# Windowed attention on one core: weighted values with the queries on the partitions, one column more for the row sums, and results that return through HBM by transposing loads

## The chip, the cores and the metric

The kernel runs on one core of one Trainium2 chip. The metric is the device time of one execution in microseconds (us), the median of several runs. All matrix operands are bf16; sums are kept in f32.

## The reference

Two attention blocks over the same x (1 x 2048 x 1024, 32 heads of 32) are mixed by a gate for each token. Block A is linear attention; block B is attention over eight earlier tokens, two apart. The change touches only block B.

```python
# block A (short): a = (phi(q) @ (phi(k)^T v)) / (phi(q) . sum phi(k)), then @ A_wo
# block B
qkv = x @ B_wqkv                         # q, k, v: 32 heads of 32
idx = pos[:, None] - 2 * arange(8)       # the token itself and 7 before it, 2 apart
logits = einsum("bhsd,bhswd->bhsw", q, k[idx]) * 32 ** -0.5   # masked where idx < 0
attn = softmax(logits)
b = einsum("bhsw,bhswd->bhsd", attn, v[idx]).reshape(B, S, D) @ B_wo
g = sigmoid((x * gate_w).sum(-1))
out = g * a + (1 - g) * b
```

## The kernel before

**Layout.** The tokens are split by parity into two halves of 1024, so that a window of stride 2 becomes eight neighbours within one half. `xT`, `qT`, `kT` hold features on the partitions (128 x 8 x 2048). `ps_all` is the whole of PSUM, eight banks of 128 x 512 f32.

**Stages.** TensorE (PE) goes through: (1) 50 warming matmuls (L1392); (2) the values of block B, x tile by x tile, each bank moved to a `vst` buffer and stored to `vB_hbm` (L1407 to L1419); (3) the keys and queries of block B, even half and then odd half (L1527 to L1543); (4) the keys of block A, `pkS` (L1577); (5) the state of block A (L1640; its small matmuls, called kv, L1627); (6) queries, fold and output, x tile by x tile (L1735 on), where one group of matmuls multiplies `qT`, which by then holds the result of block B, by `B_wo` (L1720).

**The fills.** Block B's attention is cut in 18 fills of 114 queries (two groups of 57, or 56 in the last of a half) against two groups of 64 keys. They are threaded between the big matmuls of stages 3 to 5: `slot` is called after each group of eight big matmuls, and starts a fill every fifth time (`FILL = 0.2`). A fill (`fill`, L1452) consists of:
- two loads of 64 rows of values from `vB_hbm` into a `v` buffer, one of three (L1458);
- `spread` (L1444): the queries are copied from `qT` to `qx`, for the even heads on ScalarE (ACT) and the odd heads on VectorE (DVE), with zeros elsewhere;
- **S** (L1467): 32 matmuls, 64 keys by 114 columns, into the four banks `SO` (4 to 7);
- the exponential on ACT (L1472) and the mask on DVE (L1475), both on `E`, 128 x 1824, keys on the partitions;
- three slots later **PV** (`values`, L1481): 64 matmuls (L1488) with the values as weights (64 keys x 32) and the exponentials as moving data (57 columns), and 8 matmuls (L1494) with ones as weights and 456 columns of exponentials, for the row sums; the result has head features on the partitions;
- logarithm (L1503) and exponential of the negative (L1504) of the sums on ACT, and the product on DVE (L1505), twice, each for half of the features. The product goes into `qT`, over the queries that the fill has used.

**Order.** Each operation is given to a planner (`Prog`, L63) with a cost and its dependencies. It simulates the five queues by those costs and so fixes the order of the instructions on each engine; a `move` from PSUM goes to ACT or DVE, whichever it reckons will be done first. On the chip every engine runs its list in that order, and SyncE (SP) issues nearly all DMAs, also in order.

Of the kernel before, what the change touches and what calls it, by code (L numbers as in the profile page):

```python
# [1119 lines left out]
def build_kernel(nc, A_x, A_wqkv, A_wo, B_x, B_wqkv, B_wo, gate_w, out):  # L1120
    del B_x
    S = A_x.shape[1]
# [45 lines left out]
    ps = ps_guard.__enter__()  # L1168
# [19 lines left out]

    def hb(p0, p1, half):
        return [("H%d" % half, p0, p1, None)]  # L1190

    xT = SB([128, 8, S], BF16, "xT")
    qT = SB([128, 8, S], BF16, "qT")
# [6 lines left out]
    ones = SB([128, 128], BF16, "ones")  # L1200
# [30 lines left out]
    prodr = Ring([SB([128, 1024], F32, "prod%d" % i, at=Er.t[0].lo + 4096 * i) for i in range(2)])  # L1231
# [18 lines left out]

    FILL = 0.2
    PVLAG = 3
    SUMS_AT = 2
    WARM = 50
    PASSES = 6
    mm = lambda n: max(n / 2400.0, 0.0267) + 0.0025
# [3 lines left out]
    def plan(seen):  # L1260
# [119 lines left out]
        def move(dst, src, n, bank, reg, scale=None, reads=()):  # L1380

            if scale is None:
                fd = lambda e: e.tensor_copy(dst, src())  # L1383
                fa = lambda e: e.activation(dst, src(), ACT.Copy)  # L1384
            else:
                fd = lambda e: e.tensor_scalar(dst, src(), scale, None, op0=ALU.mult)  # L1386
                fa = lambda e: e.activation(dst, src(), ACT.Copy, scale=scale)
            P.op("any", {"act": fa, "dve": fd}, {"act": act(n) + (0.1 if reads else 0.0), "dve": dps(n)}, reads=[bank.iv] + list(reads), writes=[reg])
# [9 lines left out]
        for b in range(NT // 4):  # L1398
            for half in range(2):
# [4 lines left out]
                else:  # L1404
                    steps += [[(4 * b + i, half, 0, 8)] for i in range(4)]
        open_ = {}
        for t, half, lo, hi in [p for q in steps for p in q]:  # L1407
# [8 lines left out]
            vt, vs = vst.next()  # L1416
            move(vt[:, :], bank.ap, 512, bank, vt.all())
            P.op("sp", lambda e, t=t, vt=vt, half=half: e.dma_start(vB_hbm[t * 128:(t + 1) * 128, half * 512:half * 512 + 512], vt[:, :]), 0.6, reads=[vt.all()],
                 writes=[hb(t * 128, (t + 1) * 128, half)], chan="vst%d" % vs, lat=0.5, prio=5)  # L1419
            if (t, half) in early:  # L1420
                load_w(*early[t, half], after=[o])
# [18 lines left out]
        slot_n = [0]  # L1440

        ready = []

        def spread(e_, qs, nq, offs):  # L1444
            ready.append((e_, qs))
# [6 lines left out]
        def fill(e_, qs, nq, offs):  # L1452
            t0 = e_ * HS
            k0 = [qs + nq * h - offs[h] for h in range(2)]
            m = msk[KINDS.index((nq, offs))]
            vt, vslot = vr.next()
            for h in range(2):
                P.op("sp", lambda e, h=h: e.dma_start(vt[64 * h:64 * h + 64, :], vB_hbm[t0 + k0[h]:t0 + k0[h] + 64, :]), 0.4,  # L1458
                     reads=[hb(t0 + k0[h], t0 + k0[h] + 64, i) for i in range(2)], writes=[vt.all()], chan="v%d_%d" % (vslot, h), lat=0.5)
            if (e_, qs) not in ready:  # L1460
                spread(e_, qs, nq, offs)

            def s_fn(e):
                for c in range(8):
                    for h in range(2):
                        for g in range(2):
                            last = e.matmul(SO[2 * g + c // 4].ap(c % 4 * 2 * nq, (c % 4 + 1) * 2 * nq)[64 * h:64 * h + 64, :], kT[64 * g:64 * g + 64, c, t0 + k0[h]:t0 + k0[h] + 64],  # L1467
                                            qx[64 * g:64 * g + 64, :, c, h * nq:(h + 1) * nq], start=True, stop=True, tile_position=(64 * g, 64 * h))
# [12 lines left out]
            def values():  # L1481

                def each(e):
                    for c in range(8):
                        for j in range(4):
                            for h in range(2):
                                hd = 4 * c + j
                                last = e.matmul(SO[h].ap(c * nq, (c + 1) * nq)[32 * j:32 * j + 32, :], vt[64 * h:64 * h + 64, hd * 32:hd * 32 + 32],  # L1488
                                         E[64 * h:64 * h + 64, (j // 2 * 16 + 2 * c + j % 2) * nq:(j // 2 * 16 + 2 * c + j % 2 + 1) * nq],
                                         start=True, stop=True, tile_position=(64 * h, 32 * j))  # L1490
                        if c == SUMS_AT:
                            for j in range(4):
                                for h in range(2):
                                    e.matmul(SO[2 + h].ap(0, 8 * nq)[32 * j:32 * j + 32, :], ones[64 * h:64 * h + 64, 0:32],  # L1494
                                             E[64 * h:64 * h + 64, j // 2 * 16 * nq:(j // 2 + 1) * 16 * nq].rearrange("p (c s q) -> p c s q", c=8, s=2)[:, :, j % 2, :],
                                             start=True, stop=True, tile_position=(64 * h, 32 * j))
                    return last
                bi = [s.iv for s in SO]
                P.op("pe", each, 0.66, mode="c", reads=[vt.all(), ones.all(), E.all()], writes=bi, name="PV")
                for g in range(2):  # L1500
                    L, _ = Lr.next()
                    pb = lambda o, g=g: ps[:, 4 + 2 * o:6 + 2 * o, 4 * g * nq:4 * (g + 1) * nq]
                    P.op("act", lambda e, L=L, pb=pb: e.activation(L[:, :, 0:4 * nq], pb(1), ACT.Ln), act(8 * nq), reads=[SO[2].iv, SO[3].iv], writes=[L.all()])  # L1503
                    P.op("act", lambda e, L=L: e.activation(L[:, :, 0:4 * nq], L[:, :, 0:4 * nq], ACT.Exp, scale=-1.0), act(8 * nq), reads=[L.all()], writes=[L.all()])  # L1504
                    P.op("dve", lambda e, L=L, pb=pb, g=g: e.tensor_tensor(  # L1505
                        qT[:, 4 * g:4 * g + 4, t0 + qs:t0 + qs + 2 * nq].rearrange("p c (h q) -> p h c q", h=2),
                        pb(0).rearrange("p h (c q) -> p h c q", c=4), L[:, :, 0:4 * nq].rearrange("p h (c q) -> p h c q", c=4), ALU.mult), dps(8 * nq),
                        reads=[SO[0].iv, SO[1].iv, L.all()], writes=[qT.part((4 * g, 4 * g + 4), (t0 + qs, t0 + qs + 2 * nq))])
            after(PVLAG, values)

        pace = [0.0]
# [334 lines left out]
```

## Time and profile before

| | |
|---|---|
| median of 3 runs | 484.11 us (483.94 to 484.77) |
| the profiled execution | 484.96 us, of which its span is 483.1 us |
| PE busy | 472.1 us, 98% |
| DVE busy | 304.8 us, 63% |
| ACT busy | 162.1 us, 34% |
| DMA engines, hardware queue q1 | 33.8% of 16 engines' span |
| granted TensorE clock | 1.000 |

Times in the views are microseconds from the start of the span. PE is the matmul side of TensorE, PEld its weight loads, which overlap matmuls. A matmul's duration holds its passage through the array, so that neighbours overlap: the distance of their starts is what they cost. In a row of the timeline several instructions are merged: the start of the first, the time to the end of the last, and their number; so the last one started at start + time - duration of one. `SPq` is the DMA-issuing queue of SP. In a group of instructions the numbers after the bar are busy time, mean ns of one, and the idle time before them with what ended it. Some matmul records are missing.

### The profile page before, as it was taken

What the parts mean: (1) busy time and instruction counts of PE and PEld (TensorE: products, weight loads), DVE (VectorE), ACT (ScalarE), POOL (GpSimd) and SP (SyncE); (2) the same over time, 40 slices, a digit from 0 to 9 for tenths busy, and PEclk for the clock granted to TensorE, in tenths of its full rate; (3) what the DMA queues carried; (4) which work ended last, traced back from release to release, by engine and by line L of the source; (5) the groups of instructions that cost most, each with busy time, mean ns of one, the idle gap of its engine ahead of it and who ended that gap; (6) DMA issues with size and microseconds to landing.
All of it is one profiled execution on the core that took longest, in us unless ns stands there. A gap on an engine that the chain in (4) does not pass through costs nothing.

```text
span 483.1 us, 9788 instructions
## 1 busy us (share of the span) xinstructions
PE 472.1 (98%) x4241; PEld 227.2 (47%) x4306; DVE 304.8 (63%) x514; ACT 162.1 (34%) x246; POOL 39.4 (8%) x40
## 2 busy tenths in 40 slices
PE   9999999999999999999999999999999999999997
PEld 6444444444444444444544445444444444444444
DVE  2121276799877778777743334489987777777522
ACT  1111111112344447677754466364222000011000
POOL 3000000000000000000025656010000000000000
PEclk9999999999999999999999999999999999999999
DMA  8999995232100032103004430461232111121111
GB/s 235 212 205 296 372 357 153 67 108 87 45 25 23 23 111 78 34 27 107 24 25 121 138 94 3 133 198 35 57 103 68 43 45 43 47 82 48 45 43 48
DMA packets 73973, 48.43 MB, mean 100 GB/s; under 512 B 38337, under 2 KB 67394, under 8 KB 73922
## 3 DMA queue, kind: packets, MB, share of 16 engines
q1 hardware_dynamic: 73090, 46.94, 33.8%
q10 hardware_dynamic: 832, 0.79, 0.7%
q8 instruction: 35, 0.57, 0.5%
q14 instruction: 16, 0.13, 0.1%
HBM read 30.41 MB, written 8.39 MB: 80 GB/s over the span
## 4 chain that ended last, share of the span: by engine, by line
PE 98%; issue 1%; DVE 0%
PE ps_all L1356 57%; PE ps_all L1720 23%; PE ps_all L1648 11%; PE ps_all L1467 2%; PE ps_all L1488 2%; PE ps_all L1392 1%; PE ps_all L1494 1%; PE ps_all L1627 1%; PE ps_all L1675 0%; DVE o L1386 0%
## 5 line engine op out<-in xcount | busy, mean ns | idle before, releaser
L1356 PE MATMUL ps_all<-w,xT 128*128 128x512 bf16 x493 | 109.5, 379 | 2.4 <-issue 2.1
L1356 PE MATMUL ps_all<-xT,w 128*128 128x512 bf16 x497 | 110.1, 379 | 1.6 <-issue 1.3
L1356 PEld LDWEIGHTS ps_all<-xT,w 128*128 128x128 bf16 x512 | 49.4, 98 | 58.8
L1356 PEld LDWEIGHTS ps_all<-w,xT 128*128 128x128 bf16 x512 | 49.0, 98 | 57.9
L1362 ACT ACTIVATE e<-ps_all 128x512 bf16<-128x512 f32 x64 | 38.1, 596 | 104.7 <-PE ps_all L1356 103.1
L1720 PE MATMUL ps_all<-w,qT 128*128 128x512 bf16 (+1 forms) x261 | 60.5, 373 | 0.2
L1720 PE MATMUL ps_all<-kT,aT 128*128 128x512 bf16 (+1 forms) x257 | 60.0, 372 | 0.4
L1356 PE MATMUL ps_all<-kT,xT 128*128 128x512 bf16 x249 | 57.0, 379 | 0.6 <-issue 0.3
L1648 PE MATMUL ps_all<-pk,xn 128*128 128x512 bf16 x242 | 55.5, 379 | 1.7 <-issue 1.4
L1383 DVE CAST vst<-ps_all 128x512 bf16<-128x512 f32 x16 | 11.1, 692 | 45.7 <-PE ps_all L1356 45.7
L1720 PEld LDWEIGHTS ps_all<-w,qT 128*128 128x128 bf16 x264 | 25.7, 98 | 29.7 <-issue 0.2
L1720 PEld LDWEIGHTS ps_all<-kT,aT 128*128 128x128 bf16 x264 | 25.8, 98 | 29.4
L1356 PEld LDWEIGHTS ps_all<-kT,xT 128*128 128x128 bf16 x256 | 24.7, 98 | 30.0 <-issue 0.7
L1386 DVE TENSOR_SCALAR o<-ps_all,gm 128x512 bf16<-128x512 f32 (+1 forms) x27 | 19.7, 731 | 28.0 <-PE ps_all L1720 28.0
L1648 PEld LDWEIGHTS ps_all<-pk,xn 128*128 128x128 bf16 x256 | 23.9, 98 | 27.7
L1472 ACT ACTIVATE E<-ps_all 128x1824 bf16<-128x1824 f32 (+1 forms) x18 | 30.4, 1687 | 15.8 <-PE ps_all L1467 15.8
L1505 DVE TENSOR_TENSOR qT<-ps_all,L 128x456 bf16<-128x456 f32 (+1 forms) x36 | 21.1, 625 | 20.4 <-ACT L L1504 20.2
L1363 DVE TENSOR_SCALAR e<-e 128x512 bf16<-128x512 bf16 x64 | 19.0, 299 | 23.0 <-ACT e L1362 22.8
L1610 POOL TENSOR_TENSOR zacc<-zacc,pk 128x1024 f32<-128x1024 f32 x15 | 32.0, 2131 | 17.0 <-DVE E L1475 16.2
L1384 ACT ACTIVATE vst<-ps_all 128x512 bf16<-128x512 f32 x16 | 9.6, 597 | 49.4 <-PE ps_all L1356 49.4
L1384 ACT ACTIVATE kT<-ps_all 128x512 bf16<-128x512 f32 x25 | 14.2, 600 | 31.7 <-PE ps_all L1356 31.7
L1475 DVE TENSOR_TENSOR E<-E,msk 128x1824 bf16<-128x1824 bf16 (+1 forms) x18 | 19.8, 1102 | 5.9 <-ACT E L1472 5.9
(67 smaller groups left out, 386.8 us busy)
## 6 DMA issues: line engine op xcount, KB each, us to landing
v<-vB_hbm SPq DMA_DIRECT2D x36, 128.0 KB, 2.6
vB_hbm<-vst SPq DMA_DIRECT2D x32, 128.0 KB, 4.9
w<-in_B_wqkv_dram SPq DMA_DIRECT2D x4, 1024.0 KB, 8.1
xt<-in_A_x_dram SPq DMA_DIRECT2D x16, 256.0 KB, 4.8
w<-in_A_wqkv_dram SPq DMA_DIRECT2D x4, 1024.0 KB, 9.2
xn<-in_A_x_dram SPq DMA_DIRECT2D x8, 512.0 KB, 4.1
out_dram<-o SPq DMA_DIRECT2D x15, 256.0 KB, 2.0
kT<-in_A_wqkv_dram SPq DMA_DIRECT2D x2, 1024.0 KB, 5.4
```

The costliest lines, as they stand in the source:

```text
L1356: last = e.matmul(bank.ap(), lhs(dc), rhs(dc), start=(dc == 0), stop=(dc == 7))
L1362: P.op("act", lambda e: e.activation(e_[:, :], bank.ap(), ACT.Exp), act(512), reads=[bank.iv], writes=[e_.all()])
L1363: P.op("dve", lambda e: e.tensor_scalar(e_[:, :], e_[:, :], 1.0, 1e-6, op0=ALU.min, op1=ALU.add), 0.25, reads=[e_.all()], writes=[e_.all()])
L1383: fd = lambda e: e.tensor_copy(dst, src())
L1384: fa = lambda e: e.activation(dst, src(), ACT.Copy)
L1386: fd = lambda e: e.tensor_scalar(dst, src(), scale, None, op0=ALU.mult)
L1472: P.op("act", lambda e: e.activation(E[:, 0:32 * nq].rearrange("p (j q) -> p j q", j=4), ps[:, 4:8, 0:8 * nq], ACT.Exp), act(32 * nq), rea ...
L1475: mk = P.op("dve", lambda e: e.tensor_tensor(ev(), ev(), m[:, :, :].rearrange("p r q -> p (r q)")[:, None, :].to_broadcast([128, 16, 2 * n ...
L1505: P.op("dve", lambda e, L=L, pb=pb, g=g: e.tensor_tensor(qT[:, 4 * g:4 * g + 4, t0 + qs:t0 + qs + 2 * nq].rearrange("p c (h q) -> p h c q" ...
L1610: P.op("pool", lambda e, t=t: e.tensor_tensor(zacc[:, :], zacc[:, :], pkS[:, t, :], ALU.add), 2.2, reads=[src, zacc.all()], writes=[zacc.a ...
L1648: last = e.matmul(bank.ap(), tl[:, t, cs:cs + 128], pkS[:, t, r * 512:(r + 1) * 512], start=(t == 0), stop=(t == NT - 1))
L1720: last = e.matmul(bank.ap(0, f1 - f0), lh[:, k, t * 128:(t + 1) * 128], w[:, k, f0:f1], start=(first and k == 0), stop=(not first and k == 7))
```

## The change

PV is turned round. The exponentials (64 keys x 57 queries) are now the weights, and 33 columns of values move past them: 32 of the head and one of ones, so that the row sum comes as a 33rd column and the 8 matmuls with ones go. The result has queries on the partitions. The tiles of the array are 64 x 64 (four of them) instead of 64 x 32 (eight).

For this, the eight `vst` buffers become one tile `vall` of 8 x 16 x 33 whose 33rd column is set to one once, at the start; `vB_hbm` has rows of 32 x 33, and the stores and the loads of values are longer by 1/32.

After PV, DVE takes the reciprocal of the 33rd column (128 x 32) and makes one product (128 x 1024) into a buffer `ao`, one of two; the two logarithms, two exponentials and two products go. Two stores bring `ao` to `oB_hbm` (tokens x features), and when all rows of an x tile (128 tokens) are there, `turn` issues one transposing load from it into `qT`. Stores and transposing loads are in SP's queue; a transposing load waits for the stores.

```diff
-    vB_hbm = nc.dram_tensor("vB_hbm", [S, D], BF16)
+    vB_hbm = nc.dram_tensor("vB_hbm", [S, H * 33], BF16)
+    oB_hbm = nc.dram_tensor("oB_hbm", [S, D], BF16)
...
-    vst = Ring([SB([128, 512], BF16, "vst%d" % i) for i in range(8)])
+    vall = SB([128, 8, 16, 33], BF16, "vst")
...
-    Lr = Ring([SB([128, 2, 4 * 57], F32, "L%d" % i) for i in range(2)])
-    vr = Ring([SB([128, 1024], BF16, "v%d" % i) for i in range(3)])
+    rs = SB([128, 4, 8], F32, "rs")
+    ao = Ring([SB([128, 4, 8, 32], BF16, "ao%d" % i) for i in range(2)])
+    vr = Ring([SB([128, H * 33], BF16, "v%d" % i) for i in range(3)])
...
+        P.op("dve", lambda e: e.memset(vall[:, :, :, 32:33].rearrange("p a h o -> p (a h o)"), 1.0), 0.2, writes=[vall.all()], prio=-1)
...
-            move(vt[:, :], bank.ap, 512, bank, vt.all())
+            move(vall[:, vs, :, 0:32], lambda bank=bank: bank.ap().rearrange("p (h d) -> p h d", d=32), 512, bank, vreg)
...
+        def turn(upto):
+            while (turned[0] + 1) * 128 <= upto:
+                t = turned[0]
+                turned[0] += 1
+                P.op("sp", lambda e, t=t: e.dma_start_transpose(qT[:, :, t * 128:(t + 1) * 128], oB_hbm[t * 128:(t + 1) * 128, :]), 1.4,
+                     reads=[ob(t * 128, (t + 1) * 128, i) for i in range(2)], writes=[qT.part((0, 8), (t * 128, (t + 1) * 128))], chan="ot%d" % (t % 2), lat=1.3)
...
                 def each(e):
-                    for c in range(8):
-                        for j in range(4):
-                            for h in range(2):
-                                hd = 4 * c + j
-                                last = e.matmul(SO[h].ap(c * nq, (c + 1) * nq)[32 * j:32 * j + 32, :], vt[64 * h:64 * h + 64, hd * 32:hd * 32 + 32],
-                                         E[64 * h:64 * h + 64, (j // 2 * 16 + 2 * c + j % 2) * nq:(j // 2 * 16 + 2 * c + j % 2 + 1) * nq],
-                                         start=True, stop=True, tile_position=(64 * h, 32 * j))
-                        if c == SUMS_AT:
-                            for j in range(4):
-                                for h in range(2):
-                                    e.matmul(SO[2 + h].ap(0, 8 * nq)[32 * j:32 * j + 32, :], ones[64 * h:64 * h + 64, 0:32],
...
+                    for i in range(16):
+                        for h in range(2):
+                            for g in range(2):
+                                hd = 16 * g + i
+                                c, j = hd // 4, hd % 4
+                                at = (j // 2 * 16 + 2 * c + j % 2) * nq
+                                last = e.matmul(SO[2 * h + i // 8].ap(i % 8 * 33, i % 8 * 33 + 33)[64 * g:64 * g + nq, :], E[64 * h:64 * h + 64, at:at + nq],
+                                                vt[64 * h:64 * h + 64, hd * 33:hd * 33 + 33], start=True, stop=True, tile_position=(64 * h, 64 * g))
...
+                P.op("dve", lambda e: e.reciprocal(rs[:, :, :], pv(32, 33).rearrange("p b i o -> p b (i o)")), 0.2, reads=bi, writes=[rs.all()])
+                P.op("dve", lambda e: e.tensor_tensor(o_[:, :, :, :], pv(0, 32), rs[:, :, :, None].to_broadcast([128, 4, 8, 32]), ALU.mult), dps(1024),
+                     reads=bi + [rs.all()], writes=[o_.all()])
                 for g in range(2):
-                    P.op("act", lambda e, L=L, pb=pb: e.activation(L[:, :, 0:4 * nq], pb(1), ACT.Ln), act(8 * nq), reads=[SO[2].iv, SO[3].iv], writes=[L.all()])
-                    P.op("act", lambda e, L=L: e.activation(L[:, :, 0:4 * nq], L[:, :, 0:4 * nq], ACT.Exp, scale=-1.0), act(8 * nq), reads=[L.all()], writes=[L.all()])
-                    P.op("dve", lambda e, L=L, pb=pb, g=g: e.tensor_tensor(
...
+                    P.op("sp", lambda e, g=g: e.dma_start(oB_hbm[t0 + qs:t0 + qs + 2 * nq, 512 * g:512 * g + 512].rearrange("(h q) f -> q h f", h=2),
+                                                          o_[64 * g:64 * g + nq, :, :, :].rearrange("p (h b) i d -> p h (b i d)", h=2)), 0.5,
+                         reads=[o_.all()], writes=[ob(t0 + qs, t0 + qs + 2 * nq, g)], chan="ao%d_%d" % (k, g), lat=0.5)
+                turn(t0 + qs + 2 * nq)
```

More of the change, by code (lines that the diff above doesn't have):

```diff
@@ L1190, in hb, with ob @@
         return [("H%d" % half, p0, p1, None)]
+    def ob(p0, p1, half):
+        return [("O%d" % half, p0, p1, None)]
     xT = SB([128, 8, S], BF16, "xT")
@@ L1252, in build_kernel @@
     PVLAG = 3
-    SUMS_AT = 2
     WARM = 50
@@ L1406, in plan @@
         open_ = {}
+        vn = [0]
+        P.op("dve", lambda e: e.memset(vall[:, :, :, 32:33].rearrange("p a h o -> p (a h o)"), 1.0), 0.2, writes=[vall.all()], prio=-1)
         for t, half, lo, hi in [p for q in steps for p in q]:
@@ L1415, in plan @@
                 continue
-            vt, vs = vst.next()
-            move(vt[:, :], bank.ap, 512, bank, vt.all())
-            P.op("sp", lambda e, t=t, vt=vt, half=half: e.dma_start(vB_hbm[t * 128:(t + 1) * 128, half * 512:half * 512 + 512], vt[:, :]), 0.6, reads=[vt.all()],
+            vs = vn[0] % 8
+            vn[0] += 1
+            vt = lambda vs=vs: vall[:, vs, :, :]
+            vreg = vall.part((vs, vs + 1), (0, 16), (0, 33))
+            move(vall[:, vs, :, 0:32], lambda bank=bank: bank.ap().rearrange("p (h d) -> p h d", d=32), 512, bank, vreg)
+            P.op("sp", lambda e, t=t, vt=vt, half=half: e.dma_start(vB_hbm[t * 128:(t + 1) * 128, half * 528:half * 528 + 528], vt().rearrange("p h d -> p (h d)")), 0.6, reads=[vreg],
                  writes=[hb(t * 128, (t + 1) * 128, half)], chan="vst%d" % vs, lat=0.5, prio=5)
@@ L1442, in plan @@
         ready = []
+        turned = [0]
+        def turn(upto):
[4 more added lines that the diff above has]
+                     reads=[ob(t * 128, (t + 1) * 128, i) for i in range(2)], writes=[qT.part((0, 8), (t * 128, (t + 1) * 128))], chan="ot%d" % (t % 2), lat=1.3)
         def spread(e_, qs, nq, offs):
@@ L1497, in each @@
                     return last
                 bi = [s.iv for s in SO]
-                P.op("pe", each, 0.66, mode="c", reads=[vt.all(), ones.all(), E.all()], writes=bi, name="PV")
-                for g in range(2):
[L1501 to L1508, printed above, removed]
+                P.op("pe", each, 0.6, mode="c", reads=[vt.all(), E.all()], writes=bi, name="PV")
@@ new lines, in values @@
+                o_, k = ao.next()
+                pv = lambda lo, hi: ps[:, 4:8, 0:264].rearrange("p b (i d) -> p b i d", d=33)[:, :, :, lo:hi]
+                P.op("dve", lambda e: e.reciprocal(rs[:, :, :], pv(32, 33).rearrange("p b i o -> p b (i o)")), 0.2, reads=bi, writes=[rs.all()])
+                P.op("dve", lambda e: e.tensor_tensor(o_[:, :, :, :], pv(0, 32), rs[:, :, :, None].to_broadcast([128, 4, 8, 32]), ALU.mult), dps(1024),
+                     reads=bi + [rs.all()], writes=[o_.all()])
```

2 lines of the change are left out of this document (removed).

## The prediction

> **What bounds the kernel now.** I read the busy shares and the chain first, then the groups by line, the timeline around one PV block, and the waits last.
>
> ```profile
> span 483.1 us, 9788 instructions
> PE 472.1 (98%) x4241; PEld 227.2 (47%) x4306; DVE 304.8 (63%) x514; ACT 162.1 (34%) x246; POOL 39.4 (8%) x40
> PE 98%; issue 1%; DVE 0%
> L1503 ACT ACTIVATE L<-ps_all 128x456 f32<-128x456 f32 (+1 forms) x36 | 17.8, 547 | 13.6 <-PE ps_all L1488 13.6
> L1504 ACT ACTIVATE L<-L 128x456 f32<-128x456 f32 (+1 forms) x36 | 19.0, 583 | 0.0
> L1505 DVE TENSOR_TENSOR qT<-ps_all,L 128x456 bf16<-128x456 f32 (+1 forms) x36 | 21.1, 625 | 20.4 <-ACT L L1504 20.2
> PEld ps_all L1467 <- issue: 4.7, 11, 0.4
> PEld ps_all L1488 <- issue: 3.8, 9, 0.4
> PEld ps_all L1488 <- DVE mx L1315: 2.1, 5, 0.4
> ```
>
> PE holds 98% of the chain. No wait of it is longer than 0.4 us, and those ahead of S and PV have one length whatever is named as the releaser, so they are the switch between big and small matmuls, not waiting for data. Hence time saved on ACT or DVE is worth nothing, and the 17.8 + 19.0 = 36.8 us of logarithms and exponentials that ACT loses buy nothing by themselves. What counts is how long PE needs for a PV block, and whether something new makes PE wait. I count a change of under 0.2% (0.97 us) as no change, since the runs of one kernel here lie 0.8 us apart.
>
> **The PV block before.** The first view is PE's timeline around the first PV, the second its weight loads, the third a piece of those.
>
> ```profile
> 130.99 0.81 PE L1356 MATMUL ps_all<-xT,w 128*128 128x512 bf16 x3
> 131.73 0.28 PE L1488 MATMUL ps_all<-E,v 64*32 64x57 bf16 x24
> 131.82 0.39 PE L1494 MATMUL ps_all<-E,ones 64*32 64x456 bf16 x8
> 132.03 0.51 PE L1488 MATMUL ps_all<-E,v 64*32 64x57 bf16 x40
> ...
> 131.86 0.56 PEld L1488 LDWEIGHTS ps_all<-E,v 64*32 64x32 bf16 x40
> 132.46 0.33 PEld L1356 LDWEIGHTS ps_all<-xT,w 128*128 128x128 bf16 x3
> ...
> 132.21 0.21 PEld L1488 LDWEIGHTS ps_all<-E,v 64*32 64x32 bf16 x15
> ...
> L1488 PE MATMUL ps_all<-E,v 64*32 64x57 bf16 (+1 forms) x1152 | 14.0, 191 | 0.0
> L1488 PEld LDWEIGHTS ps_all<-E,v 64*32 64x32 bf16 x1152 | 12.1, 89 | 7.9 <-issue 3.8 <-DVE mx L1315 2.1 <-DVE e L1363 0.8
> ```
>
> The last big matmul starts at 130.99 + 0.81 - 0.38 = 131.42, the first of PV at 131.73, its last at 132.03 + 0.51 - 0.19 = 132.35, and the next big weights load at 132.46. So a block is a lead of 0.31 us, a body of 0.62 us from first to last start, and a tail of 0.11 us; 18 bodies are 11.2 us, all on the path.
>
> Inside the body there are three paces. The first 24 pairs (load and matmul) start within 0.28 - 0.19 = 0.09 us, 4 ns each. The eight sums hold the array, since a tile that streams 456 columns is not free before about 0.2 us (132.03 - 131.82). The last 40 pairs are slow: their loads start between 131.86 and 132.46 - 0.04 - 0.09 = 132.33, which is 12 ns a pair with pauses, and without a pause 15 of them take 0.21 - 0.09 = 0.12 us, or 8.5 ns. Only 32 pairs went at the fast pace, and afterwards the pace is the same for every load whatever tile it is for. I read this as supply: some 32 pairs lie ready when the block starts, and later ones come from the sequencer at 8 to 12 ns a pair.
>
> **The body after.** There are 64 pairs instead of 72. The first 32 go at the array's pace, the other 32 at that of the supply. The array's pace comes from the two nearest blocks, S (64 x 64 tiles, as the new PV) and kv (32 columns moved):
>
> ```profile
> 125.91 0.60 PE L1467 MATMUL ps_all<-qx,kT 64*64 64x114 bf16 x32
> 126.44 0.33 PEld L1356 LDWEIGHTS ps_all<-xT,w 128*128 128x128 bf16 x3
> ...
> 138.51 5.13 PE L1356 MATMUL ps_all<-xT,w 128*128 128x512 bf16 x23 [0.16 <-issue]
> ...
> 262.41 0.30 PE L1488 MATMUL ps_all<-E,v 64*32 64x57 bf16 x14
> 262.64 0.37 PE L1627 MATMUL ps_all<-mT,w 128*32 128x32 bf16 x32
> 262.94 0.33 PEld L1648 LDWEIGHTS ps_all<-pk,xn 128*128 128x128 bf16 x3
> ...
> L1467 PE MATMUL ps_all<-qx,kT 64*64 64x114 bf16 (+1 forms) x576 | 10.8, 212 | 0.0
> L1627 PE MATMUL ps_all<-mT,w 128*32 128x32 bf16 x256 | 3.0, 178 | 0.0
> ```
>
> S: 32 pairs in 0.60 - 0.21 = 0.39 us, 12.6 ns each, 50 ns for a tile of its four, about what 114 columns take (48 ns) if 512 take (5.13 - 0.38) / 22 = 0.216 us. kv: 0.37 - 0.18 = 0.19 us, 6.1 ns each or 25 ns for a tile, though 32 columns would take 14. The new PV moves 33 columns through four tiles and loads 57, so 25 to 27 ns a tile, 6 to 7 ns a pair: 32 pairs in 0.21 us, by which time the supply before had also begun. Then the body is the old one less eight pairs at the supply's pace: 8 x 8.5 = 0.07 to 8 x 12 = 0.10 us; I take 0.08, since the pauses, if bound to a place in the list of instructions, stay. The tail lies between kv's 262.94 - 262.83 = 0.11 and S's 126.44 - 126.30 = 0.14, against 0.11 now: 0 taken. The lead stays.
>
> The Trainium skill ("TensorE: Matmul & The Clock Gate", section "Wait — 56ns, not 53.3ns?") says that starts never come closer than about 25 ns however few columns move. By that alone 64 matmuls would take an estimated 1.6 us and the change would lose 18 x 1.0 us. The trace agrees within a tile (kv's 25 ns) and not across tiles (24 starts in 0.09 us).
>
> So PV: 18 x -0.08 = -1.4 us. The planner's new order, as the built program shows it, also parts two more of the eight kv blocks from a neighbouring PV or S (three stand alone instead of one). Alone a kv costs its own lead, 0.31 + 0.19 + 0.11 less one big matmul's 0.22, or 0.39 us; behind PV it goes in at 262.64 - 262.52 = 0.12 us, where PV's tail would have been, and adds 0.30. That is 2 x 0.1 = +0.2 us, inside the rounding of the rest.
>
> **What the change adds elsewhere.** DVE: reciprocal and product replace two products of 625 ns.
>
> ```profile
> L1695 DVE TENSOR_TENSOR prod<-p,zb 128x1024 f32<-128x1024 bf16 x16 | 19.5, 1216 | 0.3
> L1698 DVE RECIPROCAL den<-den 128x32 f32<-128x32 f32 x16 | 5.6, 348 | 0.3
> L1315 DVE TENSOR_TENSOR mx<-mx,qT 128x1024 bf16<-128x1024 bf16 x32 | 20.8, 685 | 1.3 <-ACT qT L1387 1.2
> ...
> 292.06 1.17 DVE L1505 TENSOR_TENSOR qT<-ps_all,L 128x456 bf16<-128x456 f32 x2 [2.98 <-ACT L L1504]
> 294.28 0.50 PE L1467 MATMUL ps_all<-qx,kT 64*64 64x114 bf16 x24
> ...
> core 0: us, PE busy (x) PEld busy (x) DVE busy (x) ACT busy (x) POOL busy (x), PEclk, DMA share, GB/s
> 125.60:243.80 118.20, 114.81 (x1595) 56.81 (x1617) 91.80 (x165) 72.28 (x106) 0.00 (x0) 1.00 0.16 47
> ```
>
> By the nearest rows 0.35 + 1.22 = 1.57 us against 1.25: +0.3 us a fill, 18 x 0.3 = 5.8 us, on an engine busy 78% from 125.6 to 243.8. It costs nothing if S finds its banks free: S may start only when the product has read PSUM. Before, the products end at 293.23 and S starts at 294.28, a margin of 1.05 us with 16 big matmuls between PV and S. In the new order 15 of 17 gaps are 16 matmuls, where 13 were 24; the planner sets S closer because the chain behind PV is shorter. 16 matmuls are 3.5 us, and hand-over, reciprocal and product need 0.1 + 0.35 + 1.22 + 0.2 = 1.9, so DVE may have 1.6 us of other work in between: two maxima of 685 ns fit, three do not. Cost taken 0; bounds 0 and the rival below. The stores' columns (33 apart) leave the moves alone, as they read 512 f32 from PSUM either way.
>
> SP and DMA: two stores a fill, and 16 transposing loads that wait for them.
>
> ```profile
> vB_hbm<-vst SPq DMA_DIRECT2D x32, 128.0 KB, 4.9
> out_dram<-o SPq DMA_DIRECT2D x15, 256.0 KB, 2.0
> w<-in_B_wo_dram SPq DMA_DIRECT2D x2, 1024.0 KB, 9.1
> 30.22 0.58 SPq L1418 DMA_DIRECT2D vB_hbm<-vst  x1
> ...
> 327.64 1.24 SPq L1705 DMA_TRANSPOSE aT<-pn  x1
> ...
> 312.90 0.50 PE L1488 MATMUL ps_all<-E,v 64*32 64x56 bf16 x40
> 331.14 3.99 PE ps_all L1720 x18
> ```
>
> A store lands in 2.0 to 4.9 us, a transposing load is issued in 1.24; so SP stands still for 3 to 6 us in a fill, whose 24 + 16 big matmuls alone take 8.6. Behind it are the second halves of the value loads, needed two fills later, the loads of x, the transposes for block A's sums, and B_wo, which is the tight one. In the old order the last matmul of the last PV starts at 312.90 + 0.50 - 0.19 = 313.2; reciprocal and product (1.9), two stores' issue (two times 0.58, as a store of values takes), landing (4.9) and the transposing load (1.24) would hold SP to 322.4; B_wo would land at 331.5, and L1720 needs it at 331.14. But the new order sets the last PV 24 big matmuls (5.2 us) earlier against the fold, which leaves some 5 us. `qT` itself is wanted from 331 on. The DMA engines are 16% busy there. Cost 0.
>
> **The sum**: 484.96 (the profiled execution, span 483.1) - 1.4 + 0.2 = 483.7 in its own measure, and the same -1.2 to -1.6 on the median of 484.11: 482.7 us.
>
> **Rivals.**
> *The array alone sets the body* (the slow pairs were the sums' doing): 16 pairs a tile at 25 to 27 ns are 0.42 us, -0.2 us a block, 18 x 0.2 = 3.6: 480.7. For it, the slow pairs follow the sums; against it, they stay slow 0.3 us later. 0.10.
> *No gain*: the skill ("TensorEngine Tiling (Array Packing)", section "Instruction Overhead") says that one column takes as long as 60, so fewer columns bring nothing. In rows: kv's 25 ns a tile times 16 is 0.40 us, and the old block's columns, eight times 24 ns and the sums' 0.19, are 0.38. If the body is that plus a fixed 0.24, it stays, and the two kv blocks remain: 484.3. 0.13.
> *S waits for DVE*: if a third maximum stands ahead of the product, S is 3 x 0.685 - 1.6 = 0.45 us late. Maxima run only in the stage of keys and queries, six fills: 2.7 - 1.4: 485.4. It decides from 1.6 us of DVE work on. 0.15.
> *Pairs at S's pace*: if loading 57 columns, not 114 moving ones, set S's 12.6 ns, the body is 64 x 12.6 = 0.81, +0.19 us a block: 487.5. Against: kv's loads of 32 columns would then pace it too. 0.07.
> Other delays, mostly from SP: 0.03.
>
> **The numbers.** The forecast has 0.52, of which 0.07 falls short of 0.97 us. Faster is 0.45 + 0.10 = 0.55; same 0.07 + 0.13 = 0.20; slower 0.15 + 0.07 + 0.03 = 0.25. The range goes from the array's 480.7 to 486.2, the DVE rival with two more blocks 0.4 us late; outside lie S's pace and the rest, a little over 0.1.
>
> **What would show it.** In the new profile: L1494, L1503 and L1504 gone; PV's body near 0.54 us with its last 32 loads at 8 to 12 ns; DVE's two operations at 0.35 and 1.2 us; S's waits at 0.4 us. A body of 0.42 or 0.8, a wait of S on DVE above 0.4, or PE waiting ahead of L1720 would make it wrong.

## The result, and the profile after

The changed kernel takes 483.49 us, median of 22 runs (482.72 to 484.37); the kernel before takes 484.23 us in 22 runs (483.72 to 485.26). The ratio is 0.9982, 95% interval 0.9976 to 0.9989: 0.74 us faster, about half of the 1.4 us that was forecast. It is a gain that the runs can tell from nothing, though it is smaller than the 0.2% that the prediction set as its bound. The profiled execution took 483.49 us.

From the page of the changed kernel, the busy shares and the chain:

```profile
span 481.8 us, 9606 instructions
PE 476.6 (99%) x4162; PEld 224.9 (47%) x4162; DVE 308.9 (64%) x513; ACT 129.8 (27%) x176; POOL 39.4 (8%) x40
...
PE 99%; DVE 0%; issue 0%
```

ACT has lost 32 us and DVE has gained 4; PE still holds the whole chain. (PE's busy time can't be compared with that of before, 472.1 us, since 65 of the 4306 matmul records are missing there and none here.) The groups by line (after the bar: busy us, mean ns of one, idle time before):

```profile
L1507 PE MATMUL ps_all<-v,E 64*57 64x33 bf16 (+1 forms) x1152 | 12.4, 181 | 0.0
L1507 PEld LDWEIGHTS ps_all<-v,E 64*57 64x57 bf16 (+1 forms) x1152 | 10.6, 103 | 7.7 <-issue 4.7 <-DVE mx L1319 2.5 <-DVE e L1367 0.4
L1514 DVE RECIPROCAL rs<-ps_all 128x32 f32<-128x32 f32 x18 | 6.4, 356 | 17.2 <-PE ps_all L1507 17.2
L1515 DVE TENSOR_TENSOR ao<-ps_all,rs 128x1024 bf16<-128x1024 f32 x18 | 21.9, 1216 | 0.2
```

PV is now L1507, and the eight sum matmuls of each block are gone. Reciprocal and product take 0.356 and 1.216 us. PE's timeline and its weight loads around one PV block:

```profile
131.19 0.68 PE L1507 MATMUL ps_all<-v,E 64*57 64x33 bf16 x64
131.79 2.27 PEld L1360 LDWEIGHTS ps_all<-xT,w 128*128 128x128 bf16 x12
...
131.18 0.32 PEld L1507 LDWEIGHTS ps_all<-v,E 64*57 64x57 bf16 x32 [0.42 <-DVE mx L1319]
...
131.44 0.32 PEld L1507 LDWEIGHTS ps_all<-v,E 64*57 64x57 bf16 x28
...
161.15 0.81 PE L1507 MATMUL ps_all<-v,E 64*57 64x33 bf16 x64
```

The 64 products start within 0.68 - 0.18 = 0.50 us (0.62 before). The first 32 loads start within 0.32 - 0.10 = 0.22 us, 7 ns each; the last 28 also within 0.22 us, 8.1 ns each by these rounded rows and 8.3 by the starts in the trace. 17 of the 18 blocks are alike; the fourth, in the last row, has 0.63 us.

To see where the rest of the time went, the span is cut at two instants: the first weight load of 128 columns for the products of block B, and the last one before the end. These are the two rows of the kernel before, and then the two of the changed one:

```profile
6.61 1.46 PEld L1356 LDWEIGHTS ps_all<-w,xT 128*128 128x128 bf16 x8
...
479.40 0.10 PEld L1720 LDWEIGHTS ps_all<-kT,aT 128*128 128x128 bf16 x1
```

```profile
6.07 1.89 PEld L1360 LDWEIGHTS ps_all<-w,xT 128*128 128x128 bf16 x10
...
477.09 0.10 PEld L1733 LDWEIGHTS ps_all<-kT,aT 128*128 128x128 bf16 x1
```

| profiled run | start | first to last load | end |
|---|---|---|---|
| before | 6.61 | 472.79 | 3.7 |
| after | 6.07 | 471.02 | 4.7 |

PE's part became 1.77 us shorter, and the end, from the last weight load to the end of the span, 0.94 us longer. The start is 5.9 to 7.0 us in the fourteen profiles of this case, and differs by chance: in eight of the nine profiles with 50 warm-ups, these two among them, the first load comes as soon as the last warm-up has begun, 0.07 us behind it. The warm-ups begin 130 ns apart for the most part of the start and 71 ns apart later; that step came at 5.9 us in the profile before and at 4.7 in the one after. So the 0.54 us by which the start is shorter here are not counted for the change.

What takes longer at the end is the landing of the last store. These are the DMA views of the changed kernel and of the kernel before, each from the issue of that store to the end of the span (the first row is the busy share of the 16 DMA engines in 40 slices, in tenths; an issue row ends in us to landing):

```profile
DMA  0000009007930000000000010100000000000000
GB/s 0 0 0 0 0 0 173 0 27 233 293 92 5 0 0 0 0 0 0 0 0 0 0 11 5 11 0 16 0 0 0 0 0 0 0 0 0 0 0 0
...
q1 hardware_dynamic: 144, 0.07, 6.4%
q8 instruction: 1, 0.02, 2.7%
issues: line engine op xcount, KB each, median us to landing
out_dram<-o SPq DMA_DIRECT2D x1, 64.0 KB, 3.3
```

```profile
q1 hardware_dynamic: 144, 0.07, 8.4%
issues: line engine op xcount, KB each, median us to landing
out_dram<-o SPq DMA_DIRECT2D x1, 64.0 KB, 2.3
```

In the changed kernel one packet of queue q8, a fetch of instructions, begins behind the issue of the store. By the packet records it has 16,384 bytes, begins 1.53 us after the last weight load and takes 1.60 us, to 3.13. Most of the store's packets go in five slices about 1 us after the issue (the 173 GB/s in the seventh slice is the fetch); the last few come in slices 23 to 27, which is 3.1 to 3.6 us after the last weight load, once the fetch is over. The 2.7% of q8 are 0.43 of one engine in the 3.8 us of the window, the 1.6 us of the fetch: it holds one of the 16 engines, and the packets of the store that go to that engine wait for it. Their number says so too: of the store's 128 packets of 512 bytes, 120 begin by 2.1 us after the last weight load and eight, one engine's share, only from 3.12 on. In the kernel before the fetch began ahead of the store's issue and was over at 2.07, and again eight packets are late, but only from 2.19 on.

### The profile page after: what moved, and what is told of

Read it like the earlier page. It is cut to its first block, busy times and chain, and to the rows that moved or that the text cites. A ratio compares the mean times of both kernels' runs of the same rounds, so it can differ in the third digit from the quotient of the medians.

```text
span 481.8 us, 9606 instructions
## 1 busy us (share of the span) xinstructions
PE 476.6 (99%) x4162; PEld 224.9 (47%) x4162; DVE 308.9 (64%) x513; ACT 129.8 (27%) x176; POOL 39.4 (8%) x40
## 3 DMA queue, kind: packets, MB, share of 16 engines
q1 hardware_dynamic: 94234, 55.61, 44.3%
## 4 chain that ended last, share of the span: by engine, by line
PE 99%; DVE 0%; issue 0%
PE ps_all L1360 58%; PE ps_all L1733 23%; PE ps_all L1661 12%; PE ps_all L1507 2%; PE ps_all L1484 2%; PE ps_all L1396 1%; PE ps_all L1640 1%; PE ps_all L1688 0%; DVE o L1390 0%
## 5 line engine op out<-in xcount | busy, mean ns | idle before, releaser
L1360 PE MATMUL ps_all<-w,xT 128*128 128x512 bf16 x512 | 113.1, 379 | 0.0
L1360 PE MATMUL ps_all<-xT,w 128*128 128x512 bf16 x512 | 112.6, 379 | 0.0
L1661 PE MATMUL ps_all<-pk,xn 128*128 128x512 bf16 x256 | 57.8, 380 | 0.0
L1369 DVE SCALAR_TENSOR_TENSOR pk<-ps_all,e 128x512 bf16<-128x512 f32 x32 | 21.8, 685 | 0.7
```

The costliest lines, as they stand in the source:

```text
L1360: last = e.matmul(bank.ap(), lhs(dc), rhs(dc), start=(dc == 0), stop=(dc == 7))
L1369: P.op("dve", lambda e: e.scalar_tensor_tensor(out=dst, in0=bank.ap(), scalar=0.0, in1=e_[:, :], op0=ALU.max, op1=ALU.add), dps(512), read ...
L1661: last = e.matmul(bank.ap(), tl[:, t, cs:cs + 128], pkS[:, t, r * 512:(r + 1) * 512], start=(t == 0), stop=(t == NT - 1))
```

## The experiments

The theory after these views: PE saves some 1.75 us, because each PV block has eight pairs of weight load and matmul fewer to be supplied, and the end gives about half of it back, because the last code fetch has come to lie on the last store. Rivals: the array, not the supply, sets the block; the longer end comes from the change's own transfers; VectorE's work or the return through HBM cost something that the waits don't show.

All runs are collected in this table. The last three columns are in us, worked out from the trace as above; "fetch" is when the last 16 KB fetch that begins inside the span ran, in us after the last weight load.

| kernel | median us (runs) | ratio, 95% interval | first to last load | fetch | end |
|---|---|---|---|---|---|
| before, profiled | 484.23 (22) | | 472.79 | 0.86 to 2.07 | 3.7 |
| after, profiled | 483.49 (22) | 0.9976 to 0.9989 | 471.02 | 1.53 to 3.13 | 4.7 |
| before again | 484.13 (11) | 0.9987 to 1.0005 | 472.76 | 0.31 to 1.33 | 3.0 |
| after again | 483.87 (11) | 0.9981 to 0.9999 | 471.03 | 1.53 to 3.10 | 4.6 |
| after, no return | 481.84 (5) | 0.9938 to 0.9965 | 470.90 | -0.01 to 1.32 | 3.0 |
| before, sums last | 486.37 (5) | 1.0025 to 1.0052 | 474.91 | 0.59 to 1.77 | 3.4 |
| before, no sums | 482.01 (6) | 0.9935 to 0.9961 | 470.65 | -0.03 to 1.37 | 3.1 |
| after, 62 columns | 483.76 (11) | 0.9978 to 0.9997 | 471.19 | 1.83 to 3.08 | 4.6 |
| after, product twice | 485.46 (12) | 1.0012 to 1.0042 | 473.40 | 1.56 to 3.03 | 4.6 |
| after, 26 warm-ups | 482.04 (6) | 0.9940 to 0.9967 | 470.99 | -0.02 to 1.36 | 3.1 |
| before, 15 warm-ups | 483.87 (12) | 0.9984 to 1.0001 | 472.84 | -0.10 to 1.33 | 3.2 |
| before, 40 warm-ups | 484.26 (12) | 0.9986 to 1.0004 | 472.77 | -0.19 to 0.91 | 3.0 |
| before, 44 warm-ups | 485.35 (6) | 1.0015 to 1.0041 | 472.73 | 1.21 to 2.20 | 3.9 |
| before, 42 warm-ups | 484.08 (11) | 0.9991 to 1.0012 | 472.82 | -0.05 to 1.14 | 3.0 |

**Both kernels again, unchanged.**

> The kernel before, unchanged: a second profile and a control for the interval. In the first profiles PE's stretch (start of the first 128-column weight load to start of the last) was 472.8 us before and 471.0 after, the start ahead of it 6.6 and 6.1, the end behind it 3.7 and 4.7. Theory 1 (PE's blocks gain 1.8 us, and the end gives 0.9 back every time): the end stays at 3.7 here. Theory 2 (start and end are chance, one profile each): the end lies anywhere from 3.7 to 4.7. The ratio to the kernel before is 1 in both.

> The changed kernel, unchanged: a second profile. Theory 1: PE's stretch 471.0 again, the end 4.7 again, the median 0.7 to 0.8 us under the kernel before. Theory 2: PE's stretch 471.0, but the end anywhere from 3.7 to 4.7, and then the medians' 0.7 has another cause, such as more blocks like the fourth PV (body 0.61 us where the others have 0.50).

PE's part comes out the same within 0.03 us in both (472.76 and 471.03), and the end of the changed kernel is again 4.6, its fetch again at 1.53. So -1.75 us on PE and the late landing both belong to the kernels, not to one execution. The granted clock was 1.000 in the first profile of the changed kernel and 0.998 in this one, with PE's part and the end alike, so it is not their cause. The end of the kernel before varies with its fetch, 3.0 or 3.7. The median of the repeat, 483.87, is only 0.46 us below that session's 21 runs of the kernel before (484.33), where 0.7 to 0.8 were expected: the gain is small beside the spread of single runs.

**The return through HBM left out.**

```diff
-                for g in range(2):
-                    P.op("sp", lambda e, g=g: e.dma_start(oB_hbm[...], o_[...]), ...)
-                turn(t0 + qs + 2 * nq)
```

> The changed kernel without the stores of the results to HBM and without the transposing loads; the results of block B are left out, and the output's matmuls read the queries. If the way through HBM is hidden, as predicted: within 0.2 us of the changed kernel, PE's stretch 471.0. If it delays PE's instructions or other loads: PE's stretch shorter by 0.1 us for each hole it caused (the fourth PV), 0.5 us or more in all.

PE's part falls by only 0.12 us, and that is the fourth PV block, which is like the others here. The time falls by 1.6 us or more, where at most 0.2 was expected of a hidden return, and nearly all of it at the end. By itself this run could not say why: it takes away the transfers, but it also moves the last fetch, from 1.53 to -0.01.

**The sums behind the products, in the kernel before.**

```diff
-    SUMS_AT = 2
+    SUMS_AT = 7
```

> The kernel before with the eight matmuls for the row sums behind the 64 for the values, not after the first 24. Supply theory (32 pairs lie ready, the others come at 8.3 ns with the same two pauses): the body of a PV block stays at 0.60 us, the tail grows by up to 0.19 as the sums stream last, so 18 x 0.1 to 0.2 = 2 to 3.5 us slower or, if the pauses go, the same. Array theory (the sums in the middle cause the slow pairs): 64 pairs at 3.3 to 4 ns and the sums behind, body 0.24 to 0.29, tail 0.31: 18 x 0.13 to 0.18 = 2.3 to 3.2 us faster.

It became about 2 us slower, not faster, and PE's part 2.1 us longer. PE's timeline of a block:

```profile
132.15 0.68 PE L1488 MATMUL ps_all<-E,v 64*32 64x57 bf16 x64
...
132.64 0.43 PE L1494 MATMUL ps_all<-E,ones 64*32 64x456 bf16 x8
133.00 0.98 PEld L1356 LDWEIGHTS ps_all<-xT,w 128*128 128x128 bf16 x6 [0.21 <-issue]
```

The 64 products start within 0.68 - 0.19 = 0.49 us with all 64 in one piece, not within 0.24 to 0.29 as the array theory had it. So the products are not faster where the sums are out of their way than the supply allows. With the eight sums the loads of a block go on for 0.55 us from first to last start; and the sums, which stream 456 columns, hold up the next big load (0.21 us of waiting) when nothing follows beside which they can stream.

**The sums left out, in the kernel before.**

```diff
-                        if c == SUMS_AT:
-                            for j in range(4):
-                                for h in range(2):
-                                    e.matmul(SO[2 + h].ap(0, 8 * nq)[...], ones[...], E[...], ...)
...
-  e.activation(L[:, :, 0:4 * nq], pb(1), ACT.Ln)
+  e.activation(L[:, :, 0:4 * nq], pb(1), ACT.Copy)
```

> The kernel before with the 8 matmuls of the sums left out and ScalarE's Ln made a copy (the sums are not computed, the results are not normalized). Theory (a pair of weight load and matmul costs what its supply costs once some 32 to 40 pairs that lie ready are used up): 8 pairs fewer take 8 times 8 to 12 ns, 64 to 100 ns a block, off the 602 ns from first to last load; with two pauses of 160 ns gone as well it would be 480, as in the changed kernel; 18 blocks make 1.2 to 2.2 us, so 482.1 to 483.1. Rival (the array sets the block): the sums hold 0.2 us of it, so the block falls by 0.2 to 0.4 us or less and the time to 480.7.

```profile
131.16 0.68 PE L1488 MATMUL ps_all<-E,v 64*32 64x57 bf16 x64
131.77 2.27 PEld L1356 LDWEIGHTS ps_all<-xT,w 128*128 128x128 bf16 x12
...
131.16 0.22 PEld L1488 LDWEIGHTS ps_all<-E,v 64*32 64x32 bf16 x33 [0.42 <-DVE mx L1315]
...
131.39 0.34 PEld L1488 LDWEIGHTS ps_all<-E,v 64*32 64x32 bf16 x31
```

The same middle stretch of the loads in the kernel before, with the sums:

```profile
131.96 0.28 PEld L1488 LDWEIGHTS ps_all<-E,v 64*32 64x32 bf16 x24
```

In the old form without the sums, 57 columns through eight tiles of 64 x 32, the 64 products start within 0.49 us; in the changed kernel, 33 columns through four tiles of 64 x 64, within 0.50. The whole gain on PE is thus that of the eight matmuls that go, 2.14 us (472.79 to 470.65); turning the operands round neither brings nor costs anything in the block. The median of 482.01 also has a clear end, 3.1 us, so it is not PE's gain alone.

The loads show where the gain lies. The kernel before has two pauses in a block: 0.10 us after the 33rd load (131.86 to 131.96), and 0.06 us later on (the 24 loads of the row above end at 131.96 + 0.28 - 0.09 = 132.15, and the last 15, shown in the prediction, begin at 132.21). Without the sums the first pause stays (131.16 + 0.22 - 0.09 = 131.29 to 131.39), and the second is gone. After the first pause every load comes 8.3 ns behind the one before, 31 within 0.34 - 0.09 = 0.25 us. With the sums last, too, only the first pause is there, and by the starts in the trace the last load comes 0.547 us after the first in place of 0.481: eight pairs at 8.3 ns. So of the 0.12 us that the sums cost a block (0.602 to 0.481 from first to last load), 0.07 is their eight pairs, and the other 0.05 goes with the second pause, which only sums in the middle of the block bring. In the changed kernel the first 32 loads take 0.22 us, about as long as those of the old form and the first pause together, and from there its loads keep the same pace: so both end at 0.48.

**Nearly twice the columns, in the changed kernel.**

```diff
+                                nv = 33 if i % 8 == 7 else 62
-                                ... .ap(i % 8 * 33, i % 8 * 33 + 33) ... vt[64 * h:64 * h + 64, hd * 33:hd * 33 + 33]
+                                ... .ap(i % 8 * 33, i % 8 * 33 + nv) ... vt[64 * h:64 * h + 64, hd * 33:hd * 33 + nv]
```

> The changed kernel with 62 columns of values streamed in 56 of the 64 pairs of a PV block in place of 33 (the further columns are overwritten by the next pair, the results are the same). Theory (the new block is set by the supply of pairs, not by what the array streams): the block's 482 ns from first to last load stays within 0.05 us, the time moves by less than 0.9 us. Rival (the array's streaming sets the block: 29.5 ns for four tiles at 33 columns): 29 more columns at 0.417 ns are 12 ns more for each round of four pairs, 0.17 us for a block and 3.0 us in all: 486.7.

```profile
132.05 0.69 PE L1508 MATMUL ps_all<-v,E 64*57 64x62 bf16 x64
```

0.69 - 0.19 = 0.50 us again; PE's part grew by 0.17 us in all, where the array would have cost 3.0. The block is not set by what streams. The Trainium skill ("TensorEngine Tiling (Array Packing)", section "Instruction Overhead") has one column cost as much as 60; for 33 and 62 columns in this packed block the trace agrees.

**VectorE's product twice, in the changed kernel.**

```diff
+                P.op("dve", lambda e: e.tensor_tensor(o_[...], pv(0, 32), rs[...].to_broadcast([128, 4, 8, 32]), ALU.mult), ...)
```

> The changed kernel with VectorE's product of values and reciprocals made twice in every block, 1.2 us more of VectorE work for each of the 18. Theory (VectorE has room between the blocks, so the 0.3 us that the change adds cost nothing): less than 0.7 us slower. Rival (VectorE's work stands before the next S): each block would wait for some of the 1.2 us, up to 21 us in all; a third of it would be 7 us.

It is 1.6 to 2.0 us slower than the changed kernel, between the two expectations and outside the first. The waits of the weight loads show where (us in total, times, longest), and below them is what one of them hangs on:

```profile
PEld ps_all L1507 <- issue: 4.2, 10, 0.4
PEld ps_all L1484 <- issue: 4.2, 10, 0.4
PEld ps_all L1690 <- DVE p L1369: 3.4, 2, 2.9
PEld ps_all L1484 <- DVE mx L1319: 2.1, 5, 0.4
...
320.26 2.03 POOL L1615 COPY zb<-zr 128x1024 bf16<-128x1024 bf16 x1 [22.81 <-DMA zr<-z_hbm]
322.33 1.22 DVE L1710 TENSOR_TENSOR prod<-p,zb 128x1024 f32<-128x1024 bf16 x1 [3.14 <-POOL zb L1615]
326.69 0.14 PEld L1690 LDWEIGHTS ps_all<-kT,kvT 32*32 32x32 bf16 x16 [2.94 <-DVE p L1369]
```

S (L1484) never waits more than the 0.4 us of a switch; the fold (L1690) waits once for 2.9 us. That wait is not work piled up on DVE: ahead of `prod`, and so of the `p` behind it in its list, DVE itself stands idle for 3.14 us, until GpSimd (POOL) has copied `zb`, the sums of block A, which come back through HBM. In the changed kernel that copy begins at 310.05, ten us earlier. The planner, given the second product, laid the whole program in another order: 12 of the 17 gaps from a PV to the next S hold 24 big matmuls, 2 of 17 in the changed kernel. So this run does not isolate DVE's work: what PE lost is in the main this one wait. Only its five gaps of 16 big matmuls test the room, and there the doubled product ends 0.80 to 0.84 us ahead of S.

**The last code fetch moved away, in the changed kernel.** As many warm-up columns in fewer products shift everything behind them in PE's program, and change nothing else in it.

```diff
-    WARM = 50
+    WARM = 26
-  e.matmul(banks[7].ap(0, 156), one(128), one(156), start=True, stop=True)
+  e.matmul(banks[7].ap(0, 300), one(128), one(300), start=True, stop=True)
```

> The changed kernel with 26 warm-up products of 300 columns in place of 50 of 156: as many columns, 24 pairs of weight load and product fewer in TensorE's program, so that the point at which the last 16 KB of its code are fetched lies 24 pairs further on than in the changed kernel, where it came 17 pairs before the last product. Theory (the end gives back what the PV blocks save, since the code fetch of TensorE collides with the last store): the fetch moves away from the store, the stretch from the last weight load to the end of the span falls from 4.65 us to about 3.0, the stretch from the first to the last 128-column weight load stays at 471.0; the time is 482.1, 0.45% below the kernel before. Rival (the longer end comes from the change's own transfers or from the clock): the end stays at 4.65 us, the time at 483.5 to 483.9.

482.04 us against the 482.1 expected. The DMA view of this kernel, from the issue of the last store to the end of the span, has no row of q8 any more, and the store lands in half the time:

```profile
DMA  0000000000000001699841000000000000000000
...
q1 hardware_dynamic: 153, 0.07, 12.1%
issues: line engine op xcount, KB each, median us to landing
out_dram<-o SPq DMA_DIRECT2D x1, 64.0 KB, 1.7
```

All its transfers are those of the changed kernel, so these are not what makes the end long. Of the kernels that leave nothing out it is the fastest: ratio 0.9954 (0.9940 to 0.9967) to the kernel before, 2.3 us.

**The fetch moved in the kernel before**, with 15 products of 512 columns, 40 of 195, 44 of 178 and 42 of 186.

> The kernel before with 15 warm-up products of 512 columns in place of 50 of 156: 35 pairs fewer, so that the last code fetch ahead of the end drops out as in the changed kernel with 26 warm-up products. Theory: the end is 3.0 us in each run, the stretch 472.8, the time 483.8 (0.1% below the kernel before); the changed kernel with its fetch moved is then 1.75 us faster than this one. Rival: nothing moves, 484.2.

> The kernel before with 40 warm-up products of 195 columns in place of 50 of 156: 10 pairs fewer, so that the last code fetch falls where it falls in the changed kernel (17 pairs before the last product, not 27). Theory: the fetch meets the last store as it does in the changed kernel, the end grows from 3.0 to 3.7 us to 4.6, the stretch stays at 472.8, the time is about 485.3. Rival (the end of 4.65 belongs to the change's transfers): the end stays 3.0 to 3.7 us and the time 484.2.

> The kernel before with 44 warm-up products of 178 columns in place of 50 of 156 (as many columns, 6 pairs fewer in TensorE's program). With 40 products the last two code fetches began 0.19 us before and 3.56 us after the last weight load, either side of the last store, and the end stayed at 3.0; with 50 they began 2.87 before and 0.86 after. Theory (the end is longer where the fetch of 16 KB lies on the last store's packets, 1.76 to 2.1 us after the last weight load, whichever kernel it is): with 6 pairs fewer the last fetch begins between 1.2 and 2.0 us, the end is 4.2 to 4.7 us and the time 484.9 to 485.4. Rival (the end of 4.65 us belongs to the change's transfers): the end stays at 3.0 to 3.7, the time at 484.2.

> The kernel before with 42 warm-up products of 186 columns in place of 50 of 156 (8 pairs fewer). Theory: as with 44, the last fetch begins between 1.4 and 2.2 us after the last weight load and lies on the last store's packets, unless it has already gone past them as with 40; where it lies on them the end is 4.2 to 4.7 us and the time 484.9 to 485.4, where it doesn't 3.0 and 483.9. Rival: the end stays at 3.0 to 3.7, the time at 484.2, wherever the fetch lies.

With 15 the end is 3.2 and the time 483.87, as expected within the interval. With 40 the expectation of where the fetch would go was wrong: ten pairs fewer did not bring it from 0.86 to about 1.9 but took it out of the way, -0.19 to 0.91, with another one only after the end of the span; the end stayed at 3.0. With 42 it was the same. With 44 the fetch runs from 1.21 to 2.20, across the first packets of the store, and the kernel before becomes 1.3 us slower (interval 0.15% to 0.41%), though nothing but the warm-ups has changed; the end in the profile is 3.9, under the 4.2 to 4.7 expected. From the view of the 44 kernel, again from the store's issue to the end:

```profile
q8 instruction: 1, 0.02, 2.1%
issues: line engine op xcount, KB each, median us to landing
out_dram<-o SPq DMA_DIRECT2D x1, 64.0 KB, 2.4
```

The profiled run is the quickest of its six (484.32 us); what the fetch did in the slower ones was not seen, so that the 1.3 us come from the fetch is not shown. Over the table, whichever kernel it is: a fetch over by 1.8 us goes with an end of 3.0 to 3.4, one over at 2.1 or 2.2 with 3.7 and 3.9, one over at 3.0 to 3.1 with 4.6 and 4.7. How a program's length gives the instant of that fetch was not settled: counting pairs from the fetch before it failed for 40.

## Why the prediction was right or wrong

**That only PE's PV blocks count, and ACT's time buys nothing:** right for PE's part of the span. ACT lost 32 us, and PE's part changed by what the blocks explain. The end of the program counted too (below).

**The body, 0.54 us forecast:** it is 0.50. The reading as supply held: the first 32 pairs take 0.22 us (0.21 forecast), the later ones 8.3 ns each (8 to 12 forecast), and neither more columns nor other tiles change that. That the sequencer is what supplies them is argued and not shown; the runs show a pace that is the same whatever a pair holds. The step that was mis-sized is "eight pairs at 8.5 to 12 ns, the pauses stay". A block had 0.62 us with the sums and 0.49 without them, so the eight cost 0.12 to 0.13 us, about 16 ns each, not 0.08: besides their own supply they brought the second pause. The first one stays in the old form without them, and in the changed kernel the first 32 pairs, slower there, take up its time. All 18 PV blocks, from their first load to the next big one, went from 13.09 to 11.12 us, -1.97 where -1.4 was forecast. The rule on "Wait — 56ns, not 53.3ns?" of the Trainium skill's "TensorE: Matmul & The Clock Gate", which the prediction weighed, was rightly not followed: 64 starts in 0.50 us are 8 ns each, not 25.

**Two kv blocks alone, +0.2:** right. PE's part less the PV, S, kv and fold blocks is 446.26 us before and 446.47 after, with 2064 big matmuls in both and two switches more to small ones. (The sum with this term came to -1.2 us; the forecast of 482.7 leaves the term out.)

**DVE at no cost:** right. The waits of the weight loads in the changed kernel, to be read as before:

```profile
PEld ps_all L1484 <- issue: 5.5, 13, 0.4
PEld ps_all L1507 <- issue: 4.7, 11, 0.4
PEld ps_all L1507 <- DVE mx L1319: 2.5, 6, 0.4
...
184.80 1.21 DVE L1515 TENSOR_TENSOR ao<-ps_all,rs 128x1024 bf16<-128x1024 f32 x1
187.14 0.45 PEld L1484 LDWEIGHTS ps_all<-qx,kT 64*64 64x64 bf16 x32 [0.42 <-DVE pk L1369]
```

No S waits longer than 0.4 us, so the rival on DVE did not happen. The last two rows are the tightest of the 17 gaps: the product ends 1.13 us ahead of the next S, and up to 2.54 us in the others.

**SP, the DMAs and HBM at no cost:** right on PE's path, with 0.12 us between the changed kernel and the one without the return, and 0.2 us between 482.04 and 481.84, the two with the end clear. They did not go unnoticed:

```profile
q1 hardware_dynamic: 94234, 55.61, 44.3%
...
v<-vB_hbm SPq DMA_DIRECT2D x36, 132.0 KB, 5.0
```

The queue's share rose from 33.8% to 44.3% and the values' loads land in 5.0 us instead of 2.6; no wait of PE, ACT or DVE for them is in the profile.

**The rivals on PE:** the array alone (0.42 us) and S's pace (0.81) are both refuted by 0.50, and "no gain" by PE's 1.77 us, though in the median only 0.74 of it is left.

**What failed:** two terms of the sum, with opposite signs. The eight pairs of a block were priced at 0.08 us and cost 0.12 to 0.13. And the sum took everything ahead of the first and behind the last PV as unchanged: no term stood for the end of the program, and there the changed kernel loses 0.94 us in the profiled pair. The kernel with 26 warm-ups shows the cause: the last fetch of code lies on the last store, and the length of PE's program moves it; the one with 44 fits this without showing it. So -1.97 + 0.2 on PE and about +1 at the end give some -0.8, near the -0.74 that was measured; the end of the kernel before, 3.0 or 3.7, and the chance in the start forbid a closer account. That the time still came out at half of the forecast gain is in part luck, as the two misses work against each other. Had the end been as before, the forecast would have been too small by some 0.5 us.

## What to carry to other kernels

In a block of small packed matmuls, count pairs of weight load and matmul before columns: here each pair after the first 32 cost 8 ns whatever it streamed, and sums folded into an extra column saved eight pairs and one pause. A planner that reorders the program makes an added operation a poor test: compare the order first. When a small gain or loss doesn't match the stage that was changed, cut the span at the first and the last large instruction and compare start, middle and end apart; a change in the length of the program alone was worth 1.5 us here at the last store, more than the change under study, so two versions should be compared with that end alike.

## What the runs showed of the hardware that was not expected

The fetch of code shares the DMA engines with the data. In the trace it comes about once in 128 pairs of PE, 16,384 bytes taking 0.9 to 2.3 us (about 1.1 in the median) on one of 16 engines, and costs PE nothing that the waits show while the stream runs; at the end of the program it delayed the last store by up to 1.6 us (landing 3.3 us against 1.7). The Trainium skill ("Runtime: NRT & Kernel Launch", section "Instruction fetch mechanics") has the same blocks of 256 instructions and calls the cost of a crossing mostly hidden; the trace agrees for PE's stream and not for what shares the engine.

The fourth PV block of the changed kernel has 0.63 us in two profiles and less with 26 warm-ups or 62 columns, and it is like the others without the return or with the product made twice. The cause, worth 0.13 us, stays open.
